# Hidden rows of a bias MLP on a third engine, and the first loads on another queue

## The chip, the cores and the metric

The kernel runs on one core of one Trainium2 chip. The metric is the device time of one execution in microseconds (us), the median of three runs. The engines are PE (TensorE), PEld (its weight loads), DVE (VectorE), ACT (ScalarE), POOL (GpSimd) and SP (SyncE, which here only issues DMAs).

## The reference, cut to what matters

Attention over 2 x 8 heads of 576 positions with a bias from a small MLP on positions, then two mixture-of-experts layers on its output. What the change touches is the bias:

```python
rel = (pos[:, None] - pos[None, :]).astype(np.float32)
psi_rel = np.log1p(np.abs(rel))
psi_i = np.log1p(np.maximum(pos[:, None].astype(np.float32), 1.0))
x = (psi_rel / psi_i)[..., None]
h = np.maximum(x @ w1 + b1, 0.0)      # 32 hidden values for each (i, j)
bias = h @ w2                         # 8 heads
scores = scores + bias.transpose(2, 0, 1)[None, :, :, :]
```

After it come the softmax, the product with V and the two layers of experts (each a relu between two matrix products, weighted by probabilities).

## The kernel before

**The bias.** Psi of row i is positive, so relu(psi_rel * w1 / psi_i + b1) is relu(psi_rel * w1 + b1 * psi_i) / psi_i. A tile `T` of 128 x 576 holds psi_rel * w1 by distance, 32 hidden values for each of four rows i, and a *hidden row* (a `hid`, made by `emit_hid`, L312 to L319) is relu(T + b1 * psi_i) for four rows i: one instruction of 128 partitions by up to 576 elements. Four hidden rows, q = 0 to 3, make a *group* g of 16 rows i; there are 36 groups. For a group, PE multiplies the four hidden rows by w2 (L330; a first matmul waits for q = 0, the next for q = 1 and so on), ACT scales the product into a staging buffer `bsts` (L359, three buffers in rotation), and SP writes that to a scratch tensor `bd` in device memory (L362). From there `load_bias` (L283 to L290) reads the bias of a whole tile of scores back, shifted row by row, as `bt`.

**Where hidden rows lie.** There are 12 places for hidden rows, three groups' worth. A place comes free when PE has multiplied what it holds, so the hidden rows of the group that is m-th in order can be made once PE is done with group m - 3. The order of the groups is 0 to 7, then 32 to 35, then 8 to 31.

**The stage ahead of the first unit.** A *unit* is one tile of 128 rows of one pair of heads in one batch: scores on PE (`emit_S`, L380), bias and maximum on DVE (`emit_max`, L398), exponentials on ACT (L411), and two units later the transposes and the product with V. Before the first unit the kernel makes eight groups in a loop of eight steps, then three groups more (groups 32 to 34); each step issues a group's matmuls and copies and then the four hidden rows of the group two later. In between it splits the first queries and keys into a high and a low part (`prep_q`, `prep_k`, L232 to L235 and L253 to L254). All of it is issued in program order on every engine: no engine overtakes a waiting instruction of its own. The first unit's maximum needs its scores, which stand on PE behind group 34, and its bias, which `load_bias(0)` reads after groups 0 to 7 are written; on SP it stands behind the write of group 32.

**Which engine makes a hidden row.** `hids(k, engs)` issues k hidden rows, those with an index in `engs` on ACT and the others on DVE. In the first stage that is q = 1 on ACT and q = 0, 2, 3 on DVE; in the three groups after it all are on DVE.

**Loads.** `load_q` and `load_k` bring the queries (`qr`) and keys (`kr`), two DMAs each, issued on POOL. POOL also zeroes the last fifth of the four V tiles (L503), and during the units it adds 1e-9 to the sums (L417), spreads the reciprocals (L423) and issues the loads of V.

**The rest.** From the fourth unit on, PE is the engine that the others feed, through attention and the 96 steps of the experts.

Of the kernel before, what the change touches and what calls it, by code (L numbers as in the profile page):

```python
# [12 lines left out]
ALU = mybir.AluOpType  # L13
# [3 lines left out]
B, H, S, D = 2, 8, 576, 64  # L17
# [31 lines left out]
def attn_moe_moe(ctx: ExitStack, tc: tile.TileContext, pack, keep, rel, qT, kT, vT, w, out):  # L49
    nc = tc.nc  # L50
    pe, ve, sc, gp, sy = nc.tensor, nc.vector, nc.scalar, nc.gpsimd, nc.sync
# [131 lines left out]
    def attention(moe):  # L183
# [12 lines left out]
        b1psi = ata.tile([128, 144], F32, name="b1psi")  # L196
# [3 lines left out]
        T = ata.tile([128, S], F32, name="T")  # L200
        V = [atb.tile([128, 5, 2 * B * D], F32, name=f"V{p}") for p in range(4)]
# [10 lines left out]
        tps_ = [(t, p) for t in (0, 4, 1, 2, 3) for p in range(4)]  # L212
        units = [(t, p, b) for t, p in tps_ for b in range(2 if t < 4 else 1)]
        U = len(units)
        kk, qq, bt, rawk, rawq = {}, {}, {}, {}, {}


        def load_k(p, b):
            if b == 0:
                x = xa.tile([128, 1280], F32, tag=f"x0{XA[p]}", name=f"kr{p}")  # L220
                rawk[p, 0], rawk[p, 1] = x[:, 0:S], x[:, S:2 * S]
            for h in range(2):
                gp.dma_start(out=rawk[p, b][64 * h:64 * h + 64], in_=kT[p, b, 0:64, S * h:S * h + S])  # L223

        lows = []

        def prep_k(p, b, hi):
            r = rawk[p, b]
            kk[p, b] = ata.tile([128, 2, S], F32R, name=f"kk{p}{b}")
            h = kk[p, b][:, 0, :]  # L230
            if hi is sc:
                sc.activation(out=h, in_=r, func=AF.Copy)  # L232
            else:
                ve.tensor_copy(h, r)
            lows.append(lambda: ve.tensor_tensor(out=kk[p, b][:, 1, :], in0=r, in1=h.bitcast(F32), op=ALU.subtract))  # L235

        def prep_lows():
            while lows:
                lows.pop(0)()

        def load_q(t, p):
            r = ata.tile([128, 256], F32, tag="qraw", name=f"qr{t}{p}", bufs=4)
            for h in range(2):
                gp.dma_start(  # L244
                    out=r[64 * h:64 * h + 64].rearrange("p (b c) -> p b c", b=2),
                    in_=qT[t, p, 0:64].rearrange("p (b h c) -> p h b c", b=2, h=2)[:, h],
                )
            rawq[t, p] = r

        def prep_q(t, p):  # L250
            r = rawq[t, p]
            a = ata.tile([128, 2, 256], F32R, tag="qq", name=f"qq{t}{p}", bufs=3)
            ve.tensor_copy(a[:, 0, :], r)  # L253
            ve.tensor_tensor(out=a[:, 1, :], in0=r, in1=a[:, 0, :].bitcast(F32), op=ALU.subtract)  # L254
            qq[t, p] = a
# [13 lines left out]
        def load_bias(i):  # L269

            t, p = tps_[i]
            n = 128 if t < 4 else 64

            src = bdram[t][2 * p:2 * p + 2].rearrange("h i v -> h (i v)")
            o = S - 1 - 128 * t
            src = src[:, o:o + n * (W - 1)].rearrange("h (i v) -> i h v", v=W - 1)[:, :, 0:S]
            at = [slice(n * z, n * z + n) for z in range(1 if t < 4 else 2)]
            if place[i] < 2:
                x = two[place[i]]
                bt[t, p] = x[:, 0:S], x[:, S:2 * S]  # L280
                mains, tails = x.rearrange("p (h c) -> p h c", h=2)[:, :, 0:512], x[:, 512:640].rearrange("p (h c) -> p h c", h=2)
                for z in at:
                    sy.dma_start(out=mains[z], in_=src[:, :, 0:512])  # L283
                    sy.dma_start(out=tails[z], in_=src[:, :, 512:S])
            else:
                x0, x1 = bt[t, p] = third
                for z in at:
                    sy.dma_start(out=x0[z], in_=src[:, 0, :])
                    sy.dma_start(out=x1[z, 64:S], in_=src[:, 1, 0:512])
                    sy.dma_start(out=x1[z, 0:64], in_=src[:, 1, 512:S])  # L290
# [6 lines left out]
        def ranges(g):  # L297
            fwd, rev = S - 16 * g, 16 * g + 16
            n = max(fwd, rev)
            return fwd, rev, n, 1 if n <= 512 else 2  # L300
# [5 lines left out]
        def emit_hid(g, eng, q):  # L306
            tt = 4 * g + q
            if started == 6:
                for i in XA[4:]:
                    x = xa.tile([128, 1280], F32, tag=f"x0{i}", name=f"hid{i}")  # L310
                    free.extend([(6, x[:, 0:S]), (6, x[:, S:2 * S])])
            place = free.pop(0)  # L312
            taken[g, q], x = place, place[1]
            n = ranges(g)[2]
            if eng is ve:
                ve.tensor_scalar(x[:, 0:n], T[:, 0:n], b1psi[:, tt:tt + 1], 0.0, op0=ALU.add, op1=ALU.max)
            else:
                sc.activation(out=x[:, 0:n], in_=T[:, 0:n], func=AF.Relu, bias=b1psi[:, tt:tt + 1])
            hid[g, q] = x  # L319
# [165 lines left out]
        kq = [(p, b) for p in range(4) for b in range(2)]  # L485
# [7 lines left out]
        busy(WARM)  # L493
        sy.dma_start(out=cst, in_=pack)
        sc.dma_start(out=T, in_=rel)
        load_q(*tps_[0])
        load_k(*kq[0])
        load_k(*kq[1])
        sy.dma_start(out=kept, in_=keep)
        load_q(*tps_[1])  # L500
        load_k(*kq[2])
        for p in range(4):
            gp.memset(V[p][:, 4, :], 0.0)  # L503
        ve.tensor_scalar(b1psi, cst[:, C_PSI:C_PSI + 144], b1col, None, op0=ALU.mult)
        ve.tensor_scalar(w2n, cst[:, C_W2:C_W2 + 32], 8.0, None, op0=ALU.mult)
        ve.tensor_scalar(T, T, w1col, None, op0=ALU.mult)
# [2 lines left out]
        order = list(range(8)) + list(range(32, NGR)) + list(range(8, 32))  # L509
        made = 0  # L510
        started = 0

        def hids(k, engs=()):
            nonlocal started
            for i in range(k):
                if started < 4 * NGR and (free or started == 6):
                    emit_hid(order[started // 4], sc if i in engs else ve, started % 4)
                    started += 1

        def groups(k):  # L520
            nonlocal made
            for _ in range(k):
                if made < NGR:
                    g = order[made]
                    emit_bias_out(g, emit_bias_mm(g))
                    made += 1

        FIRST = 8
        hids(8, (1, 5))
        for g in range(FIRST):  # L530
            groups(1)
            if g == 0:
                prep_q(*tps_[0])
            if g == 1:
                prep_k(*kq[0], ve)
                prep_lows()
            hids(4, (1,))
            if g == 3:
                load_k(*kq[3])
            if g == 4:  # L540
                prep_k(*kq[1], ve)
                prep_lows()
            if g == 6:
                load_k(*kq[4])
                load_q(*tps_[2])
# [2 lines left out]
        load_q(*tps_[3])  # L548
        prep_q(*tps_[1])
        prep_k(*kq[2], sc)  # L550
        for g in range(3):
            groups(1)
            hids(4)
            prep_lows()
            if g == 0:
                load_bias(0)
                load_bias(1)
# [7 lines left out]
        for k in range(U + 3):  # L565
            first = False
            if k < U:
                t, p, b = units[k]
# [398 lines left out]
    with tc.manual_schedule():  # L967
        attention(moe)
        moe.run()
# [69 lines left out]
```

## Time and profile before

| | |
|---|---|
| median of three runs | 1348.43 us (1348.18 to 1350.22) |
| span of the profiled execution | 1346.6 us |
| time around the span (median less span) | 1.8 us |
| PE busy | 1332.0 us, 99% of the span |
| DVE, ACT, POOL busy | 783.9, 519.0 and 434.2 us |

The span runs from the first to the last instruction of the profiled execution; its own time is that span, and the runs' median stands 1.8 us above it. A busy share of 99% for PE is over the whole span: the first 40 us are the stretch in which PE waits for others, and they are the stretch that the change touches.

### The profile page before, as it was taken

Reading aid. Unit: us, or ns where it says so; the run is one execution under the profiler, and the core shown is the slowest. Engines: PE = TensorE matmul, PEld = TensorE weight load, DVE = VectorE, ACT = ScalarE, POOL = GpSimd, SP = SyncE. Lnnn points to the kernel's source line nnn. Section 1 sums busy time; section 2 is a strip of 40 time slices with the busy share of each in tenths; the row PEclk is TensorE's granted clock in tenths of the full one; section 3 lists DMA queues with packets and bytes.
Section 4 is the critical chain, followed back from the end, with each engine's and each line's share of the span. In section 5 each row is a group of like instructions: output and inputs, shape, how many; then the busy total and the mean of one; then the engine's idle time right before and its main releaser. Section 6 shows DMA issues by size and latency. Waiting matters only on the chain.

```text
span 1346.6 us, 22479 instructions
## 1 busy us (share of the span) xinstructions
PE 1332.0 (99%) x8783; PEld 1163.1 (86%) x8783; DVE 783.9 (58%) x1771; ACT 519.0 (39%) x1230; POOL 434.2 (32%) x455
## 2 busy tenths in 40 slices
PE   8999999999999999999999999999999999999998
PEld 4677888898898988898898988998988898989887
DVE  7888977463564653765763654644735725645533
ACT  6888863341331422443342421422422413313311
POOL 4633433260440530361440530620612603504400
PEclk9999999999999999999999999999999999999999
DMA  7975421020120210020110110210210200202010
GB/s 220 240 199 145 143 64 63 32 94 1 38 88 1 63 64 1 32 75 21 63 63 1 63 63 1 80 47 1 94 32 30 92 5 32 95 0 63 32 40 32
DMA packets 34314, 84.68 MB, mean 63 GB/s; under 512 B 8864, under 2 KB 9120, under 8 KB 34208
## 3 DMA queue, kind: packets, MB, share of 16 engines
q1 hardware_dynamic: 31184, 75.60, 18.0%
q0 software_dynamic: 2880, 7.34, 2.0%
q8 instruction: 69, 1.13, 0.3%
q14 instruction: 37, 0.30, 0.1%
q10 hardware_dynamic: 144, 0.29, 0.1%
HBM read 69.97 MB, written 13.25 MB: 62 GB/s over the span
## 4 chain that ended last, share of the span: by engine, by line
PE 92%; DVE 3%; POOL 2%; issue 2%; ACT 1%; DMA 0%; SPq 0%; ACTq 0%; POOLq 0%; DVEq 0%
PE y L778 43%; PE B L699 17%; PE A L699 11%; PE C L699 11%; PE po L469 3%; PE sc L380 2%; PE tp L443 2%; PE bps L330 1%; POOL kr L223 1%; POOL qr L244 1%; DVE rows L800 0%; PE sc L431 0%; PE turn L867 0%; DMA rawb<-in_w 0%; DVE h L713 0%
## 5 line engine op out<-in xcount | busy, mean ns | idle before, releaser
L778 PE MATMUL y<-gb,h 128*128 128x512 f32 x2592 | 714.1, 395 | 0.0
L778 PEld LDWEIGHTS y<-gb,h 128*128 128x128 f32 x2592 | 450.2, 188 | 55.3
L169 POOL TENSOR_TENSOR gb<-rawb,gb 128x512 fp32r<-128x512 f32 x94 | 122.9, 1322 | 627.9 <-ACT gb L168 624.9
L707 DVE TENSOR_TENSOR u<-B,s 128x320 f32<-128x320 f32 (+1 forms) x192 | 87.8, 457 | 333.4 <-PE B L699 333.4
L710 ACT ACTIVATE h<-c 128x320 fp32r<-128x320 f32 (+1 forms) x288 | 119.7, 439 | 368.5 <-DVE c L707 367.1
L713 DVE SCALAR_TENSOR_TENSOR h<-c,h 128x320 fp32r<-128x320 f32 (+1 forms) x288 | 182.4, 650 | 53.7 <-ACT h L710 49.4
L169 POOL TENSOR_TENSOR ga<-rawa,ga 128x512 fp32r<-128x512 f32 x94 | 127.2, 1371 | 4.3 <-ACT ga L168 2.7
L169 POOL TENSOR_TENSOR ga<-wt,ga 128x512 fp32r<-128x512 f32 x94 | 107.3, 1161 | 24.5 <-ACT ga L168 15.7
L707 DVE TENSOR_TENSOR c<-C,u 128x320 f32<-128x320 f32 (+1 forms) x192 | 87.1, 454 | 37.7 <-PE C L699 33.9
L721 ACT ACTIVATE s<-A 128x320 f32<-128x320 f32 (+1 forms) x96 | 39.4, 411 | 165.6 <-PE A L699 165.3
L168 ACT ACTIVATE gb<-rawb 128x512 fp32r<-128x512 f32 x96 | 60.1, 627 | 86.0 <-DMA rawb<-in_w 86.0
L710 ACT ACTIVATE h<-A 128x320 fp32r<-128x320 f32 (+1 forms) x96 | 38.9, 405 | 137.9 <-PE A L699 137.8
L707 DVE TENSOR_TENSOR c<-B,s 128x320 f32<-128x320 f32 (+1 forms) x96 | 43.9, 457 | 73.9 <-PE B L699 72.7
L699 PE MATMUL B<-x20S,ga 128*128 128x320 f32 x384 | 66.9, 310 | 0.0
L699 PE MATMUL A<-x20A,ga 128*128 128x320 f32 x384 | 66.8, 309 | 0.0
L699 PE MATMUL C<-x20S,ga 128*128 128x320 f32 x384 | 66.7, 309 | 0.0
L699 PEld LDWEIGHTS C<-x20S,ga 128*128 128x128 f32 x384 | 61.4, 188 | 5.9 <-DVE c L707 0.2
L699 PEld LDWEIGHTS A<-x20A,ga 128*128 128x128 f32 x384 | 61.5, 188 | 5.7
L699 PEld LDWEIGHTS B<-x20S,ga 128*128 128x128 f32 x384 | 61.5, 188 | 5.8
L411 ACT ACTIVATE s<-s,stat 128x576 f32<-128x576 f32 x72 | 55.7, 774 | 18.8 <-DVE stat L398 18.6
L699 PEld LDWEIGHTS C<-x21S,ga 128*128 128x128 f32 x384 | 54.6, 188 | 8.1 <-DVE c L707 2.7
L699 PEld LDWEIGHTS A<-x21A,ga 128*128 128x128 f32 x384 | 54.7, 188 | 5.5
(183 smaller groups left out, 1915.5 us busy)
## 6 DMA issues: line engine op xcount, KB each, us to landing
rawa<-in_w SPq DMA_DIRECT2D x48, 512.0 KB, 4.0
rawb<-in_w SPq DMA_DIRECT2D x48, 512.0 KB, 4.9
bd<-bsts SPq DMA_DIRECT2D x36, 295.5 KB, 3.6
bt<-bd SPq DMA_DIRECT2D x13, 512.0 KB, 4.7
qr<-in_qT POOLq DMA_DIRECT2D x40, 64.0 KB, 3.2
kr<-in_kT POOLq DMA_DIRECT2D x16, 144.0 KB, 4.4
V<-in_vT POOLq DMA_DIRECT2D x4, 512.0 KB, 7.3
out<-rows SPq DMA_DIRECT2D x8, 256.0 KB, 2.1
```

The source lines that it names most:

```text
L168: sc.activation(out=z(0), in_=src, func=AF.Copy)
L169: lo.tensor_tensor(out=z(1), in0=src, in1=z(0).bitcast(F32), op=ALU.subtract)
L380: pe.matmul(out=o[h][c:c + n, j, 0:288], lhsT=a[d, 128 * bb + c:128 * bb + c + n], rhs=m[d, 288 * j:288 * j + 288], start=t == 4 or i == 0 ...
L411: sc.activation(out=s, in_=s, func=AF.Exp, scale=-1.0, bias=stat[u][:, h:h + 1], accum_out=stat[u][:, 2 + h:3 + h],)
L443: pe.transpose(o[:, j, :], s[:, 640 * h + 128 * j:640 * h + 128 * j + 128], ident)
L469: pe.matmul(out=o[64 * h:64 * h + 64, c0:c0 + n], lhsT=V[p][:, j, col:col + D], rhs=rhs, start=j == 0, stop=j == 4,)
L699: pe.matmul(out=ban[o], lhsT=a, rhs=x[:, z, k, :], start=not more and i == 0, stop=i == 5, skip_group_check=more,)
L707: ve.tensor_tensor(out=t[o], in0=ban[a], in1=t[b], op=ALU.add)
L710: sc.activation(out=h[f][:, 0, half, :], in_=src, func=AF.Relu)
L713: ve.scalar_tensor_tensor(out=h[f][:, 1, half, :], in0=src, scalar=0.0, in1=h[f][:, 0, half, :].bitcast(F32), op0=ALU.max, op1=ALU.subtract,)
L721: sc.activation(out=t["s1"], in_=ban["A"], func=AF.Copy)
L778: pe.matmul(out=self.y[t], lhsT=a, rhs=x, start=g == 0 and f == 0 and i == 0, stop=g == NP - 1 and f == 1 and i == 2,)
```

## The change

Four edits, all ahead of the first unit.

- Hidden rows: of every eight in a row, numbers 0 and 4 (q = 0 of every group) are made by POOL, number 5 (q = 1 of every second group) by ACT, and the other five by DVE. This goes for the first 52 hidden rows, the three last groups of the stage included.
- `load_q` and `load_k` take a queue as an argument, and the first two queries and the first three keys are issued on SP in place of POOL.
- The zeroing of V's last fifth is issued after the loop of eight steps in place of before it.
- Later loads stay on POOL, where they now stand between its hidden rows.

```diff
-        def load_k(p, b):
+        def load_k(p, b, q=gp):
...
-                gp.dma_start(out=rawk[p, b][64 * h:64 * h + 64], in_=kT[p, b, 0:64, S * h:S * h + S])
+                q.dma_start(out=rawk[p, b][64 * h:64 * h + 64], in_=kT[p, b, 0:64, S * h:S * h + S])
...
-        def load_q(t, p):
+        def load_q(t, p, q=gp):
...
-            if eng is ve:
-                ve.tensor_scalar(x[:, 0:n], T[:, 0:n], b1psi[:, tt:tt + 1], 0.0, op0=ALU.add, op1=ALU.max)
+            if eng is not sc:
+                eng.tensor_scalar(x[:, 0:n], T[:, 0:n], b1psi[:, tt:tt + 1], 0.0, op0=ALU.add, op1=ALU.max)
...
-        load_q(*tps_[0])
-        load_k(*kq[0])
-        load_k(*kq[1])
+        load_q(*tps_[0], sy)
+        load_k(*kq[0], sy)
+        load_k(*kq[1], sy)
         sy.dma_start(out=kept, in_=keep)
-        load_q(*tps_[1])
-        load_k(*kq[2])
-        for p in range(4):
-            gp.memset(V[p][:, 4, :], 0.0)
+        load_q(*tps_[1], sy)
+        load_k(*kq[2], sy)
...
-        def hids(k, engs=()):
+        def hids(k, three=False):
...
-                    emit_hid(order[started // 4], sc if i in engs else ve, started % 4)
+                    eng = {0: gp, 5: sc, 4: gp}.get(started % 8, ve) if three else ve
+                    emit_hid(order[started // 4], eng, started % 4)
...
-        hids(8, (1, 5))
+        hids(8, True)
...
-            hids(4, (1,))
+            hids(4, True)
...
+        for p in range(4):
+            gp.memset(V[p][:, 4, :], 0.0)
         for g in range(3):
             groups(1)
-            hids(4)
+            hids(4, True)
```

On POOL, from the start of the program to the first unit, the rows before were these (`qr`, `kr` are queries and keys, `V` the V tiles):

```order
L487 MEMSET ones 128x128
L244 DMA qr_126<-in_qT 64x2x128 x2
L223 DMA kr_129<-in_kT 64x576 x4
L244 DMA qr_135<-in_qT 64x2x128 x2
L223 DMA kr_138<-in_kT 64x576 x2
L503 MEMSET V_100 128x256
...
L223 DMA kr_138<-in_kT 64x576 x2
L223 DMA kr_270<-in_kT 64x576 x2
L244 DMA qr_273<-in_qT 64x2x128 x2
L223 DMA kr_270<-in_kT 64x576 x2
L244 DMA qr_290<-in_qT 64x2x128 x2
```

Now the later part of them, from the seventh hidden row to the last of the stage, reads so (`hids` and `hidS` are places of hidden rows):

```order
L223 DMA kr_138<-in_kT 64x576 x2
L316 TENSOR_SCALAR hids<-T,b1psi 128x480
L316 TENSOR_SCALAR hids<-T,b1psi 128x464
L316 TENSOR_SCALAR hidS_151<-T,b1psi 128x528
L223 DMA kr_266<-in_kT 64x576 x2
L244 DMA qr_269<-in_qT 64x2x128 x2
L316 TENSOR_SCALAR hids<-T,b1psi 128x544
L223 DMA kr_266<-in_kT 64x576 x2
L244 DMA qr_286<-in_qT 64x2x128 x2
L551 MEMSET V_100 128x256
...
L316 TENSOR_SCALAR hids<-T,b1psi 128x560
```

Ten DMA issues have left the head of POOL's queue, 13 hidden rows have come into it, and the q = 0 row of group 34 (the 128x560 one) now stands behind eight DMA issues and four memsets that follow the row of group 32 (128x528), with only the row of group 33 (128x544) between.

On SP, the start of the program (`cst` holds the constants, `kept` the identity and gate weights):

```order
 L494 DMA cst<-in_pack 128x214
+L244 DMA qr_126<-in_qT 64x2x128 x2
+L223 DMA kr_129<-in_kT 64x576 x4
 L499 DMA kept<-in_keep 128x196
+L244 DMA qr_135<-in_qT 64x2x128 x2
+L223 DMA kr_138<-in_kT 64x576 x2
 L362 DMA bd_104<-bsts 16x8x591 x8
```

Ten issues have come ahead of the first write of a group; from that write on SP's rows are those of before.

## Rows read from the trace of the kernel before

**Rows 1.** The page's first line.

```profile
span 1346.6 us, 22479 instructions
```

**Rows 2.** Windows: length, busy PE, PEld, DVE, ACT, POOL, then PE's clock.

```profile
4.80:28.60 23.80, 19.62 (x166) 8.46 (x165) 22.20 (x52) 18.18 (x34) 11.03 (x19) 0.93 0.71 205
...
39.50:330.00 290.50, 289.41 (x2607) 239.83 (x2608) 203.23 (x552) 180.06 (x447) 102.59 (x163) 1.00 0.38 109
```

**Rows 3.** Timeline of DVE: start, length, instruction [idle before it and releaser].

```profile
31.10 0.76 DVE L398 CUSTOM_DVE_ANT_0 s<-sc,bt 128x576 f32<-128x576 f32 x1 [2.60 <-DMA bt<-bd]
```

**Rows 4.** Timelines of SP, ACT and PE ahead of it.

```profile
26.46 0.39 SPq L283 DMA_DIRECT2D bt<-bd  x1
...
18.78 1.05 ACT L359 ACTIVATE bsts<-bps,cst 128x496 f32<-128x496 f32 x2 [0.99 <-DMA bd<-bsts]
...
20.45 0.93 PE L330 MATMUL bps<-hids,w2n 128*32 128x464 f32 x1 [1.55 <-ACT hids L318]
```

**Rows 5.** DVE's groups of instructions by line, 4.8 to 28.6 us.

```profile
L316 DVE TENSOR_SCALAR hidS<-T,b1psi 128x560 f32<-128x560 f32 (+6 forms) x21 | 9.4, 506 | 0.0
L316 DVE TENSOR_SCALAR hids<-T,b1psi 128x448 f32<-128x448 f32 (+7 forms) x21 | 9.3, 495 | 0.3 <-PE bps L330 0.3
```

**Rows 6.** Timeline of DVE and, last, of POOL.

```profile
6.88 1.18 DVE L316 TENSOR_SCALAR hidS<-T,b1psi 128x560 f32<-128x560 f32 x2
...
14.86 1.22 DVE L316 TENSOR_SCALAR hids<-T,b1psi 128x480 f32<-128x480 f32 x3
...
17.54 0.82 DVE L316 TENSOR_SCALAR hidS<-T,b1psi 128x464 f32<-128x464 f32 x2
...
22.62 0.93 DVE L316 TENSOR_SCALAR hidS<-T,b1psi 128x560 f32<-128x560 f32 x2
...
26.96 1.54 DVE L316 TENSOR_SCALAR hids<-T,b1psi 128x448 f32<-128x448 f32 x4
...
7.16 1.80 POOL L503 MEMSET V<- 128x256 f32 x4
```

**Rows 7.** POOL's arithmetic by line, whole span: shortest, median and longest, ns.

```profile
L417 POOL TENSOR_SCALAR stat<-stat x36: 203/213/798, 33.6 to 178.2; 128x2 f32<-128x2 f32 x36
L423 POOL COPY spread<-stat x36: 287/290/697, 38.7 to 178.7; 128x128 f32<-128x128 f32 x36
L169 POOL TENSOR_TENSOR gb<-rawb,gb x94: 1275/1298/1572, 154.4 to 1259.2; 128x512 fp32r<-128x512 f32 x94
```

**Rows 8.** The same view of a DVE line in the experts.

```profile
L713 DVE SCALAR_TENSOR_TENSOR h<-c,h x288: 412/492/1575, 189.0 to 1336.3; 128x320 fp32r<-128x320 f32 x72, 128x256 fp32r<-128x256 f32 x72
L713 DVE SCALAR_TENSOR_TENSOR h<-A,h x96: 407/445/492, 186.4 to 1331.5; 128x320 fp32r<-128x320 f32 x48, 128x256 fp32r<-128x256 f32 x48
```

**Rows 9.** POOL's groups of instructions by line, 0 to 16 us.

```profile
L223 POOL DMA_DIRECT2D kr<-in_kT x12 | 7.2, 605 | 0.0
L244 POOL DMA_DIRECT2D qr<-in_qT x8 | 5.7, 711 | 0.4 <-issue 0.4
```

**Rows 10.** Timeline of PE: end of group 5, start of group 34, first scores.

```profile
15.90 0.59 PE L330 MATMUL bps<-hidS,w2n 128*32 128x496 f32 x3
...
25.53 0.43 PE L330 MATMUL bps<-hids,w2n 128*32 128x280 f32 x2 [0.39 <-ACT bsts L359]
...
28.59 1.06 PE L380 MATMUL sc<-kk,qq 64*128 64x288 f32 x12
```

**Rows 11.** Windows, columns as in rows 2.

```profile
16.50:20.40 3.90, 1.10 (x9) 0.23 (x8) 3.90 (x10) 2.85 (x7) 0.00 (x0) 1.00 0.73 240
20.40:24.00 3.60, 3.55 (x24) 0.86 (x24) 2.81 (x7) 3.21 (x8) 0.00 (x0) 0.53 0.64 170
```

**Rows 12.** DMA issues at 10 to 12 and 23 to 25 us, last: us to landing.

```profile
bd<-bsts SPq DMA_DIRECT2D x1, 295.5 KB, 5.6
...
bd<-bsts SPq DMA_DIRECT2D x1, 295.5 KB, 3.0
```

**Rows 13.** POOL's sequencer in the chain that ended last.

```profile
15.82 0.06 POOLq L417 x2
```

More of the change, by code (lines that the diff above doesn't have):

```diff
@@ L239, in prep_lows @@
                 lows.pop(0)()
-        def load_q(t, p):
+        def load_q(t, p, q=gp):
             r = ata.tile([128, 256], F32, tag="qraw", name=f"qr{t}{p}", bufs=4)
             for h in range(2):
-                gp.dma_start(
+                q.dma_start(
                     out=r[64 * h:64 * h + 64].rearrange("p (b c) -> p b c", b=2),
```

## The prediction

> **What bounds the kernel now.** I read the stages first (windows), then asked what the first unit waits for (DVE's timeline at the first maximum), and followed that wait back through the timelines of SP, ACT and PE. From 39.5 us on PE is busy 289.41 of the next 290.50 us; in the stage that makes the bias, 4.8 to 28.6 us, only 19.62 of 23.80 [rows 2]. So a shift of the first unit should move the end one for one, and nothing else that the change does can move it. The first maximum starts at 31.10, after 2.60 us in which DVE waits for the bias `bt` [rows 3]. Back from there: SP issues that load at 26.46, once group 7 is written; group 7's first matmul starts at 20.45, after a wait of 1.55 us for its hidden row on ACT; and that row stands on ACT behind the copy of group 5, which starts at 18.78 because its staging buffer is still being written out [rows 4]. DVE, busy 22.20 of 23.80 us [rows 2], is the busiest engine of the stage, but it is not what group 7 waited for: its last row of that group ended at 17.54 + 0.82 = 18.36 [rows 6]. DVE's share looks like the bound; the waits say it has some 2 us of slack.
>
> **What a POOL row takes.** The trace has no such instruction on POOL. The nearest with one input: 128x2 takes 213 ns, the copy of 128x128 290 ns (medians), 0.61 ns an element, so 0.21 + 574 x 0.61 = 0.56 us for 576 elements as the lower bound. The nearest of this length has two inputs: 1.30 us for 512, 1.46 for 576, the upper bound [rows 7]. I take 0.85, nearer to the copy, since the row has one input, and above it, since it does two operations on each element. By the Trainium skill (GPSIMD Engine Reference, "Elementwise — side-by-side cycle accounting") a tight loop on POOL does 1.8 cycles an element at 1.2 GHz, an estimate of 0.86 us and some 0.2 of start, by which the sum below would come out about 1 us later.
>
> **What it takes from DVE.** Two DVE rows of 128x560 took 1.18 us while POOL's memsets ran, 0.93 with POOL idle: 0.13 lost per row beside a memset of 0.45 [rows 6]. In the experts, DVE's instruction with both inputs in SBUF goes from 412 to 1575 ns, its twin with one input in PSUM never beyond 492 [rows 8], and beside it run POOL's subtractions of 1.3 us; a 128x2 operation of POOL that takes 203 ns at best took up to 798 [rows 7]. So the two engines hold something from each other. I charge DVE what POOL's row has beyond its start (0.85 - 0.2 = 0.65), less about 0.1 of DVE's own start that passes meanwhile, as with the memsets: 0.55 a row, bounds 0.25 and 1.15 by the two ends above.
> By the Trainium skill (SBUF — State Buffer, "Who interferes with whom") DVE's two-port operations, tensor_scalar among them, and a POOL operation share one port pair, and whoever comes second waits for the whole instruction. The rows on both sides agree. With the whole 0.85 charged, DVE below would be ready at 33.7 in place of 29.8 and the prediction 1351.0.
>
> **DVE's account up to the first maximum.** Before, 42 of the 52 hidden rows are DVE's (21 + 21) [rows 5], and its last one ends at 26.96 + 1.54 = 28.50 [rows 6]. After, numbers 0 and 4 of each eight give POOL 13, number 5 gives ACT 6 (10 before), and DVE keeps 33. Nine rows less at 0.40 each (four of 128x448 in 1.54, four of 128x560 in about twice 0.93 less overlap: a start every 0.36 to 0.42 [rows 6]) is -3.6. Thirteen POOL rows at 0.55 is +7.2. The memsets and DMA issues that stood beside some five of the early rows, 0.13 each, go: -0.7. Some 1.6 us in which DVE was idle [rows 2] take up the same amount. 28.5 - 3.6 + 7.2 - 0.7 - 1.6 = 29.8, before 31.1: not the bound. The bounds give 25.9 and 37.6.
>
> **The bias.** Through group 7, POOL makes 8 rows, DVE 20 in place of 24: 8 x 0.55 - 4 x 0.40 - 0.7 = +2.1, so DVE is done with group 7 at 20.5, when PE began it before (20.45). Its matmuls then ran at a clock of 0.53 [rows 11]. ACT gives up every second row but keeps group 7's. The write of group 7 took 3.0 us with no load beside it, that of group 1, among POOL's loads, 5.6 [rows 12]; the loads now stand later, near group 7. I take no net change for `bt`: 0, bounds -2.5 and +2.6.
>
> **POOL's queue.** This is the new path. PE's first scores come behind group 34, whose q = 0 row stands on POOL behind eight DMA issues and four memsets. Start: PE was done with group 5 at 15.90 + 0.59 = 16.5 [rows 10], and POOL's row of group 32 needs that. DVE's rows of group 5 ended at about 14.9, when those of group 6 began [rows 6]; now 6 x 0.55 - 3 x 0.40 - 0.7 = 1.4 later, 16.3, and PE 1.0 after it: 17.3. Then three POOL rows at 0.85 + 0.2 of waiting for DVE, 3.2; four issues for keys at 0.605 and four for queries at 0.711 [rows 9], 5.3; four memsets at 0.45 [rows 6], 1.8: group 34's row is there at 27.6. From the start of group 34 to the end of the first scores PE took 28.59 + 1.06 - 25.53 = 4.1 us [rows 10]: 31.7, which is 0.6 later than the 31.1 of before. And PE has then idled some 4 us. Before, it was busy 1.10 of 3.90 us from 16.5 and ran the next 3.60 us at a clock of 0.53, close to the 1.2 GHz level [rows 11]; if that comes again, 1.7 of the 4.1 us is done twice as slowly. I take most of it, 1.4: 33.1, +2.0 against 31.1. Bounds: with the short row, no waiting for DVE and full clock, 28.2, and `bt` decides; with the long row, group 5 at 19.9, 6.0 for the rows, 5.3, 1.8, 4.1 and 1.7, 38.8: +7.7.
>
> **What costs nothing.** SP's ten new issues, at about the 0.39 us of its load at 26.46 [rows 4], end near 6 us, ahead of its first write of a group, which no hidden row made after 4.8 can reach before 7. The early queries and keys are on DVE's list after its first six hidden rows, so 2 us of DVE's work covers them; if that were gone, a late key would hold DVE. V's zeroing is wanted only in the units; its 1.8 us is charged on POOL above.
>
> **The sum.** The profiled execution is 1346.6 us of span [rows 1], the median 1348.43, 1.8 around the span. 1346.6 + 2.0 = 1348.6 of span, 1350.4 by the median. A measurement here can tell about 0.2%, 2.7 us, from no change.
>
> **The rivals.**
> 1. *Faster: the waits for the staging buffers go.* Before, the copy of group 5 started at 18.78, 0.99 us late for its buffer [rows 4]; without POOL's loads among the writes (5.6 to 3.0 [rows 12]) group 7 comes up to 1.9 earlier, and 0.6 more at full clock. It decides if a POOL row costs DVE no more than it saves, 0.40, and POOL's queue reaches group 34 by 24.5. For it speaks the POOL row at the copy's rate; against it, the queue's 7.1 us of issues and memsets. 1348.4 - 2.2 = 1346.2.
> 2. *Nothing moves*: DVE's and POOL's accounts both end below 31.1 and `bt` lands as before, 1348.4. It needs the clock to stay up at group 34.
> 3. *DVE and POOL in series.* A POOL row nearer to 1.3 us: DVE's account ends near 36 and POOL's queue near 38, 1355. For it speaks that all long POOL rows in the trace are at that rate, against it that they have two inputs.
> 4. *POOL starts late.* Its sequencer has two instructions at 15.82 [rows 13] ahead of its first arithmetic, and no work for 17 us after, so a start-up could hide there; now its first row is wanted where the stage starts, at 4.8 [rows 2], and nothing hides it. If it takes until 7, the first group is 2.1 us late; POOL has little slack to make it up: up to 1352.5. The Trainium skill (GPSIMD Engine Reference, "Instruction dispatch") gives the first call after a library is loaded about 6 us; no row here shows it.
>
> **How the numbers follow.** The forecast, a POOL queue that makes the first scores 0.5 to 4.5 us late, 0.45 (its own range 1348.9 to 1352.9); rival 1, 0.17; rival 2, 0.15; rival 3, 0.16; rival 4, 0.07. The range leaves out about half of rivals 1 and 3: 1346.4 to 1354.8. Faster by over 0.2% is half of rival 1, 0.08. Slower by over 0.2% is 0.18 of the forecast (2.7 to 4.5 us late), rival 3 and most of rival 4: 0.39. The rest, 0.53, is within 0.2%.
>
> **What would show it.** Right: POOL's L316 rows near 0.85 us; DVE's rows beside them stretched by half a microsecond; PE waiting on POOL ahead of group 34, a clock near 0.5 after it, and the first maximum released by PE's scores near 33 with the same 1.8 us around the span. Wrong: DVE's rows as short as before beside POOL's; the first maximum still released by `bt`; PE waiting on POOL at the first groups (rival 4); or POOL rows of 1.3 us.

## The result, and the profile after

The changed kernel takes 1362.03 us (median of 5 runs, 1361.04 to 1362.31); the kernel before, run beside it, 1350.22 (1348.18 to 1351.74). The ratio is 1.0091, with a 95% interval of 1.008 to 1.0102 (estimated from the runs, so not quite the quotient of the two medians): slower by 0.9%, some 12 us. Against the 1348.15 and 1348.44 us that the kernel before has in the experiments below it is 13.6 to 13.9 us. The profiled execution has a span of 1360.5 us, 13.9 more than [rows 1].

The first maximum on DVE, the row that answers to [rows 3], in DVE's timeline of the changed kernel (start, length, instruction, idle before it and its releaser):

```profile
44.38 0.76 DVE L398 CUSTOM_DVE_ANT_0 s<-sc,bt 128x576 f32<-128x576 f32 x1 [7.37 <-PE sc L380]
```

It starts 13.3 us later than before, so nearly all of the 13.9 us is lost ahead of it. It is released by PE's scores and no longer by the bias `bt`. The two stages ahead of it, as windows with the columns of [rows 2], the first being that of [rows 2]:

```profile
4.80:28.60 23.80, 15.35 (x116) 3.91 (x115) 22.32 (x35) 11.83 (x23) 23.77 (x15) 0.71 0.53 145
28.60:39.50 10.90, 3.65 (x32) 1.20 (x32) 5.62 (x8) 2.55 (x5) 10.86 (x13) 0.53 0.90 250
```

POOL is busy 23.77 of 23.80 us (11.03 before) and 10.86 of the next 10.90. PE is busy 15.35 us in the first stage (19.62 before) and runs at a clock of 0.71, then 0.53 (the 1.2 GHz level is 0.5). The waits up to 55 us (engine and line, what it waited for, us in total, times, longest) say who waits for POOL:

```profile
PE bps L330 <- POOL hids L316: 13.9, 6, 4.3
...
PE bps L330 <- POOL hidS L316: 1.6, 3, 0.7
...
DVE hids L316 <- PE bps L330: 3.9, 2, 2.8
```

POOL's timeline shows why. It answers to [rows 6, 7, 9]:

```profile
4.78 5.35 POOL L316 TENSOR_SCALAR hids<-T,b1psi 128x576 f32<-128x576 f32 x2 [3.85 <-DVE T L504]
10.11 2.68 POOL L316 TENSOR_SCALAR hidS<-T,b1psi 128x544 f32<-128x544 f32 x1
12.77 4.53 POOL L316 TENSOR_SCALAR hids<-T,b1psi 128x528 f32<-128x528 f32 x2
17.29 2.14 POOL L316 TENSOR_SCALAR hidS<-T,b1psi 128x496 f32<-128x496 f32 x1
...
20.70 3.87 POOL L316 TENSOR_SCALAR hids<-T,b1psi 128x480 f32<-128x480 f32 x2
24.55 2.24 POOL L316 TENSOR_SCALAR hidS<-T,b1psi 128x528 f32<-128x528 f32 x1
26.75 1.17 POOL L223 DMA_DIRECT2D kr<-in_kT  x2
27.91 1.29 POOL L244 DMA_DIRECT2D qr<-in_qT  x2
29.23 3.01 POOL L316 TENSOR_SCALAR hids<-T,b1psi 128x544 f32<-128x544 f32 x1
32.20 1.11 POOL L223 DMA_DIRECT2D kr<-in_kT  x2
33.30 1.20 POOL L244 DMA_DIRECT2D qr<-in_qT  x2
34.49 1.08 POOL L551 MEMSET V<- 128x256 f32 x4
35.55 2.29 POOL L316 TENSOR_SCALAR hids<-T,b1psi 128x560 f32<-128x560 f32 x1
37.84 2.20 POOL L316 TENSOR_SCALAR hidS<-T,b1psi 128x576 f32<-128x576 f32 x1
40.02 1.77 POOL L316 TENSOR_SCALAR hids<-T,b1psi 128x448 f32<-128x448 f32 x1
```

From 4.78 us on POOL runs without a gap; nothing releases its rows but its own queue. A row takes 1.77 to 3.0 us, on average 2.31 over the 13 (the ten groups come to 30.1 us). The last two ran after DVE had made its last hidden row of the stage: alone, 576 elements take 2.20 us and 448 take 1.77. For the mean length of the 13 rows, 524 elements, that gives an estimate of 2.03 us, so most of the length is POOL's own and some 0.3 us a row comes from running beside DVE. The row of group 34 (128x560) is done at 35.55 + 2.29 = 37.84. PE's timeline from there, which answers to [rows 10] (L491 are products that the kernel makes only to keep PE busy, before as after), and the same stretch as a window with the columns of [rows 2]:

```profile
37.90 0.68 PE L330 MATMUL bps<-hids,w2n 128*32 128x280 f32 x2 [3.56 <-POOL hids L316]
...
39.92 3.43 PE L491 MATMUL po<-ones 128*128 128x128 f32 x16
...
43.28 1.06 PE L380 MATMUL sc<-kk,qq 64*128 64x288 f32 x12
```

```profile
37.90:44.34 6.44, 6.44 (x45) 4.73 (x45) 0.00 (x0) 1.59 (x3) 3.89 (x2) 0.62 0.64 170
```

From group 34's start to the end of the first scores PE takes 43.28 + 1.06 - 37.90 = 6.44 us, 2.3 more than the 4.12 of before: its matmuls take 0.68 where they took 0.43, after 3.56 us without work, and the clock of the stretch is 0.62 where it was 1.00 (25.53 to 29.65 us before). DVE's groups from 4.8 to 43 us answer to [rows 5] (busy us, mean ns of one):

```profile
L316 DVE TENSOR_SCALAR hidS<-T,b1psi 128x560 f32<-128x560 f32 (+6 forms) x18 | 12.9, 766 | 0.3 <-PE bps L330 0.3
L316 DVE TENSOR_SCALAR hids<-T,b1psi 128x576 f32<-128x576 f32 (+6 forms) x15 | 10.0, 712 | 3.9 <-PE bps L330 3.9
```

33 rows take 22.9 us, 0.69 each; before it was 42 in 18.7, 0.445 each. So 22.9 - 33 x 0.445 = 8.2 us is lost, 0.63 for each of 13 POOL rows, or 0.75 for each of the 11 that had rows of DVE beside them. It is not what ends the stage: DVE itself waits 3.9 us here.

### The profile page after: what moved, and what is told of

Its sections match the earlier page's. It is cut to its first block, busy times and chain, and to the rows that moved or that the text cites. A ratio compares the mean times of both kernels' runs of the same rounds, so it can differ in the third digit from the quotient of the medians.

```text
span 1360.5 us, 22499 instructions
## 1 busy us (share of the span) xinstructions
PE 1335.4 (98%) x8783; PEld 1162.6 (85%) x8783; DVE 792.9 (58%) x1762; ACT 516.9 (38%) x1226; POOL 456.4 (34%) x458
## 4 chain that ended last, share of the span: by engine, by line
PE 91%; DVE 5%; POOL 2%; ACT 1%; issue 1%; DMA 1%; SPq 0%; ACTq 0%; DVEq 0%; POOLq 0%
PE y L779 42%; PE B L700 16%; PE C L700 11%; PE A L700 11%; PE po L469 3%; PE sc L380 2%; PE tp L443 2%; PE bps L330 2%; POOL hids L316 1%; DVE wt L165 1%; DVE h L714 1%; PE po L491 1%; POOL hidS L316 0%; DVE rows L801 0%; PE sc L431 0%
```

## The experiments

**The theory, A**: a hidden row on POOL is some 2.7 times as long as the prediction took it; 13 of them in order, with the eight DMA issues and four memsets between, make POOL the bound of the stage, and its last row ahead of group 34 sets the first scores. **The rivals**: that the loads moved to SP or the late zeroing cost the time; that DVE's loss beside POOL does, or the rows that ACT no longer makes; that the POOL row is long only for its place or its operands; that PE's idle clock carries the loss; and that the plan would lose with short rows too.

**1. No hidden rows on POOL.** The rows are dealt out to DVE and ACT as before; the loads on SP and the late zeroing stay.

```diff
-                    eng = {0: gp, 5: sc, 4: gp}.get(started % 8, ve) if three else ve
-                    emit_hid(order[started // 4], eng, started % 4)
+                    emit_hid(order[started // 4], sc if i in engs else ve, started % 4)
...
-        hids(8, True)
+        hids(8, (1, 5))
...
```

> Hidden rows as before (q = 1 on ACT, the others on DVE), the moved loads and the later zeroing kept. Theory A (POOL's 13 hidden rows at 2.2 to 3.0 us each are the whole loss): the first maximum returns to about 31 us or a little ahead, the time is 1346 to 1350 us. Rival B (the loads on SP or the late zeroing carry a part of the 12 us): over 1353 us.

Measured: 1348.86 us against 1348.15, ratio 1.0005 (0.9994 to 1.0016). DVE's timeline has the first maximum a little earlier than before:

```profile
30.13 0.76 DVE L398 CUSTOM_DVE_ANT_0 s<-sc,bt 128x576 f32<-128x576 f32 x1 [2.75 <-DMA bt<-bd]
```

The loads and the zeroing cost nothing that can be measured. The 1.0 us by which the first unit comes earlier is nearly all given back: the span is 1346.3 us, 0.3 less.

**2. The hidden rows alone.** The opposite: POOL has its 13 rows, and the loads and memsets stand at the head of its queue again.

```diff
-        load_q(*tps_[0], sy)
-        load_k(*kq[0], sy)
-        load_k(*kq[1], sy)
+        load_q(*tps_[0])
+        load_k(*kq[0])
+        load_k(*kq[1])
...
+        for p in range(4):
+            gp.memset(V[p][:, 4, :], 0.0)
...
-        for p in range(4):
-            gp.memset(V[p][:, 4, :], 0.0)
```

> Only POOL's hidden rows: all loads back on POOL, the zeroing back ahead of the stage. Theory A (POOL's queue in series): ten loads and the zeroing stand ahead of POOL's first row, which comes at about 9 us in place of 4.8; the 1.1 us of late zeroing goes; first maximum 46 to 48 us, time 1363 to 1367 us. Rival B (the moved loads hurt): 1355 us or less.

Measured: 1363.42 us, ratio 1.0107 (1.0091 to 1.0122), the first maximum on DVE at 45.82:

```profile
45.82 0.76 DVE L398 CUSTOM_DVE_ANT_0 s<-sc,bt 128x576 f32<-128x576 f32 x1 [7.28 <-PE sc L380]
```

The rows alone bring the whole loss; clearing POOL's queue ahead of them gives 1.4 us of the first maximum back.

**3. What a row on POOL takes, by form.** Behind the last output tile of the kernel before, with the other engines idle, POOL does eight forms on 128x512 from SBUF to SBUF, twice (`sx` and `so` are 128x512, `col` is a column: one value for each partition).

```diff
...
+        for _ in range(2):
+            gp.tensor_scalar(so, sx, col, 0.0, op0=ALU.add, op1=ALU.max)
+            gp.tensor_scalar(so, sx, col, None, op0=ALU.add)
+            gp.tensor_scalar(so, sx, 0.5, 0.0, op0=ALU.add, op1=ALU.max)
+            gp.tensor_scalar(so, sx, 0.5, None, op0=ALU.add)
+            gp.tensor_scalar(so, sx, 0.0, None, op0=ALU.max)
+            gp.tensor_scalar(so, sx, 0.5, 0.25, op0=ALU.mult, op1=ALU.add)
+            gp.tensor_copy(so, sx)
+            gp.tensor_tensor(out=so, in0=sx, in1=sx, op=ALU.add)
```

> The kernel before, with eight forms of a POOL instruction of 128x512 appended after the last output tile, each twice, on idle engines: two operations with a column operand (the hidden row's form), one operation with a column, two and one with constants, a maximum alone, multiply-add with constants, a copy, a sum of two inputs. From POOL's rows that ran alone after the change (2.20 us for 576, 1.77 for 448) the first form takes 1.98 us. Theory C1 (the second operation costs): the one-operation forms take about half, 1.0 to 1.2 us, with or without the column. Theory C2 (the column operand costs): the forms with constants take 1.0 to 1.2 and one operation with a column about 2. Theory C3 (every tensor_scalar on POOL costs this): all near 2 us, the copy 0.5 to 0.6. The time has no meaning beside the kernel before but for some 20 us at its end.

Measured, POOL's timeline, in the order of the diff (the second round differs by 0.01 at most):

```profile
1346.80 2.01 POOL L974 TENSOR_SCALAR forms<-rows,kept 128x512 f32<-128x512 f32 x1 [76.61 <-DVE rows L800]
1348.91 1.58 POOL L975 TENSOR_SCALAR forms<-rows,kept 128x512 f32<-128x512 f32 x1
1350.58 1.92 POOL L976 TENSOR_SCALAR forms<-rows 128x512 f32<-128x512 f32 x1
1352.59 1.49 POOL L977 TENSOR_SCALAR forms<-rows 128x512 f32<-128x512 f32 x1
1354.16 1.49 POOL L978 TENSOR_SCALAR forms<-rows 128x512 f32<-128x512 f32 x1
1355.73 0.62 POOL L979 TENSOR_SCALAR forms<-rows 128x512 f32<-128x512 f32 x1
1356.42 0.61 POOL L980 COPY forms<-rows 128x512 f32<-128x512 f32 x1
1357.11 1.04 POOL L981 TENSOR_TENSOR forms<-rows 128x512 f32<-128x512 f32 x1
```

The row's own form takes 2.01 us with every other engine idle, so its length needs neither its place in the stage nor DVE beside it. None of the three explanations came out as stated: the column in place of a constant costs 0.09 us and the second operation 0.43, but one addition or one maximum by itself already takes 1.49, while a multiplication and an addition together take 0.62, a copy's time. Why POOL has a fast and a slow kind, no run here shows.

**4. Half the rows.** POOL makes the first of every eight, 7 in all, and DVE the rest.

```diff
-                    eng = {0: gp, 5: sc, 4: gp}.get(started % 8, ve) if three else ve
+                    eng = {0: gp, 5: sc}.get(started % 8, ve) if three else ve
```

> One hidden row of eight on POOL in place of two (7 in place of 13), DVE takes the others. Theory A (POOL's queue in series): up to group 34 it has 6 rows x 2.3 + 10 issues x 0.62 + 1.1 of zeroing = 21 us from 4.8, so group 34's row is there at 26, first scores at 30 to 31; the time is 1347 to 1352 us. Rival D (any row on POOL holds DVE for all of its 2.2 us, whatever the queue): DVE, 39 rows x 0.41 + 7 x 2.2 + 4 of splits from 4.8, ends at 40, the time is 1357 us or more.

Measured: 1352.71 us, ratio 1.0031 (1.0022 to 1.0041), the first maximum at 34.88, some 4 us later than theory A said and far below its rival. PE still waits for POOL, twice, for 6.5 us:

```profile
PE bps L330 <- POOL hids L316: 6.5, 2, 4.5
```

A's direction holds and its number was too low: group 34 starts on PE at 29.11, when POOL's row is there, and not at 26, and from there to the end of the first scores PE takes 5.7 us in place of 4.12, at a clock of 0.70 (29.1 to 34.8 us).

**5. The five later loads off POOL's queue.** All 13 rows stay on POOL; SP issues these loads too.

```diff
-                load_k(*kq[3])
+                load_k(*kq[3], sy)
...
-        load_k(*kq[5])
-        load_q(*tps_[3])
+        load_k(*kq[5], sy)
+        load_q(*tps_[3], sy)
```

> The changed kernel with its 13 hidden rows on POOL, and the five loads that stood between them issued on SP as well. Theory A (POOL's queue in series): the eight issues of 1.2 to 1.3 us a pair, 6.0 us up to group 34's row, leave the queue; the first maximum comes at about 38 to 39 in place of 44.4, the time is 1355 to 1358 us. Rival E (the issues were hidden, and POOL's rows wait for PE's places or for DVE instead): 1360 us or more.

Measured: 1357.05 us, ratio 1.0061 (1.0046 to 1.0076), the first maximum at 39.51, 4.9 us earlier than in the changed kernel. Ten issues are off the queue; the eight ahead of group 34's row had taken 4.8 us there (1.17 + 1.29 + 1.11 + 1.20 in the timeline above), so what leaves the queue leaves the time. The rest of the loss stays with the rows.

**6. A cheap form.** POOL's 13 rows as the fast form of experiment 3; their relu is left out.

```diff
+            if eng is gp:
+                gp.tensor_scalar(x[:, 0:n], T[:, 0:n], 1.0, b1psi[:, tt:tt + 1], op0=ALU.mult, op1=ALU.add)
...
```

> The changed kernel with POOL's 13 rows in the form of a multiplication by 1 and an addition of the column: the relu is left out of those rows. On idle engines such a form with constants took 0.62 us for 512 in place of 2.01. Theory A with the prediction's own sum (only the price of a row was wrong): at 0.65 to 0.9 us a row the first maximum comes at 30.5 to 33, the time is 1347.5 to 1351 us. Rival F (the number of POOL rows and their hold on DVE matter, not their length): 1356 us or more.

Measured: 1348.34 us against 1348.44, ratio 1.0002 (0.9992 to 1.0011). POOL's rows by source line (shortest, median, longest, ns):

```profile
L316 POOL TENSOR_SCALAR hids<-T,b1psi x9: 735/910/1088, 4.7 to 25.3; 128x560 f32<-128x560 f32 x2, 128x576 f32<-128x576 f32 x1, 128x528 f32<-128x528 f32 x1, 128x512 f32<-128x512 f32 x1
...
L316 POOL TENSOR_SCALAR hidS<-T,b1psi x4: 816/865/907, 6.6 to 24.5; 128x544 f32<-128x544 f32 x1, 128x496 f32<-128x496 f32 x1, 128x528 f32<-128x528 f32 x1, 128x576 f32<-128x576 f32 x1
```

That is about the 0.85 us that the prediction took, in the same place beside the same work, and the loss is gone: the length of the row is the whole cause. ACT's rows are those of the changed kernel, so they are not the cause, and DVE's loss beside short rows is not either. The plan also gains nothing with short rows. DVE's timeline and the chain, in order of time, say what decides then:

```profile
32.80 0.76 DVE L400 CUSTOM_DVE_ANT_0 s<-sc,bt 128x576 f32<-128x576 f32 x1 [3.32 <-DMA bt<-bd]
```

```profile
22.36 6.19 DMA bd<-bsts
...
28.75 0.39 SPq L283 DMA_DIRECT2D bt<-bd  x1
```

Group 34's row is done at 24.46 and no longer decides; `bt` does, as before, but its load is issued at 28.75 in place of 26.46, behind a write of the bias that takes 6.2 us (3.0 before [rows 12]). POOL's loads now run beside that write; that they are what makes it longer is my reading, and no run takes them away with these rows. The first maximum is 1.7 us later in this execution, whose span (1348.9) belongs to the longest of the ten runs; in the median of the ten nothing of it shows, and I leave that open.

**7. Half the rows, loads first.** Experiment 4 with POOL's five later loads at the head of its queue.

```diff
+        load_k(*kq[3])
+        load_k(*kq[4])
+        load_q(*tps_[2])
+        load_k(*kq[5])
+        load_q(*tps_[3])
...
```

> One row in eight on POOL, and the five later loads at the head of POOL's queue, ahead of its first row, the zeroing behind. Theory A: POOL's queue is 7.7 us of loads, then 5 rows x 2.4, 1.1 to 1.6 of zeroing and group 34's row, which is there at 24 to 25; the first maximum waits for the bias again, 30 to 32, the time is 1347 to 1350 us, no better than before. Rival G (a POOL row costs DVE more than it saves): the maximum later than 33, over 1351 us.

Measured: 1350.53 us, ratio 1.0012 (1.0002 to 1.0021), the first maximum at 32.55 and released by PE's scores:

```profile
32.55 0.76 DVE L398 CUSTOM_DVE_ANT_0 s<-sc,bt 128x576 f32<-128x576 f32 x1 [1.10 <-PE sc L380]
```

A little above what theory A said, and not by its path: the first maximum does not wait for the bias. POOL's row of group 34 is done at 23.00 + 2.42 = 25.42, and what PE then waits for is DVE, whose last rows of that group end at 27.12 + 1.23 = 28.35 (22.62 + 0.93 = 23.55 before [rows 6]). POOL's and DVE's timelines:

```profile
23.00 2.42 POOL L316 TENSOR_SCALAR hids<-T,b1psi 128x560 f32<-128x560 f32 x1 [0.43 <-PE bps L330]
```

```profile
27.12 1.23 DVE L316 TENSOR_SCALAR hidS<-T,b1psi 128x560 f32<-128x560 f32 x2
```

The chain runs back from there over DVE's rows and PE's first groups to POOL's first row, which the loads ahead of it put at 7.21 us in place of 4.78. So this run lies between theory A and rival G. Seven slow rows don't pay even with every load out from between them.

**8. PE kept busy ahead of groups 33 and 34.** The changed kernel, with idle matmuls (`busy`) on PE while it waits for POOL.

```diff
         for g in range(3):
+            if g:
+                busy(14)
             groups(1)
```

> The changed kernel with 14 more warm-up products on PE ahead of group 33 and ahead of group 34 (some 3.6 us each, while PE would wait for POOL). Theory A with a clock term: PE, no longer idle, keeps its 2.4 GHz level, group 34 to the end of the first scores takes 4.1 to 4.5 us in place of 6.4, the first maximum comes at 42 to 42.5, the time is 1358.5 to 1360.5 us. Rival H (the clock has no part, POOL's queue alone sets the end): unchanged at 1362 us, or later.

Measured: 1359.93 us, ratio 1.0088 (1.0072 to 1.0105); the span is 1357.6 us, 2.9 less than that of the changed kernel. PE's timeline, and the window from the start of group 34 to the end of the first scores:

```profile
37.68 0.43 PE L330 MATMUL bps<-hids,w2n 128*32 128x280 f32 x2
...
40.74 1.06 PE L380 MATMUL sc<-kk,qq 64*128 64x288 f32 x12
```

```profile
37.68:41.80 4.12, 4.12 (x46) 3.17 (x45) 0.00 (x0) 1.58 (x3) 3.65 (x2) 1.00 0.87 224
```

Group 34 starts 0.2 us earlier than in the changed kernel and its first scores end 40.74 + 1.06 - 37.68 = 4.12 us later, as long as before the change. The clock there is 1.00 in place of 0.62. So 6.44 - 4.12 = 2.3 us of the loss is the clock to which PE had fallen while it waited, and the rest, 11.5 us by this run (1359.93 against 1348.44), stays with POOL's queue.

## Why the prediction was wrong

**The step that failed is "What a POOL row takes".** It took 0.85 us, with bounds of 0.56 and 1.46; measured are 2.20 us alone for 576 elements and 2.31 on average in the stage, where the rows are 448 to 576 elements long. The bounds came from the nearest rows, a copy and a subtraction of two inputs, and experiment 3 shows that neither bounds an addition and a maximum: a copy of 512 takes 0.61, the two-input addition 1.04, the row's form 2.01. "Nearer to the copy, since the row has one input" ordered the forms by their inputs, and POOL doesn't. The estimate by the Trainium skill (GPSIMD Engine Reference, "Elementwise — side-by-side cycle accounting"), 0.86 us and some start, was too short in the same way; the measurement decides.

**"POOL's queue" was the right path with one wrong term.** Group 32's row started at 24.55, not 17.3, because the POOL rows ahead of it end only there; the three rows took 2.24 + 3.01 + 2.29 = 7.5 us in place of 3.2; the eight issues 4.8 (5.3) and the memsets 1.1 (1.8). Together 37.84 for group 34's row, where I had 27.6: 10.2 us, all of it row length, since the other two terms were too dear by 1.2. Behind it stand 6.4 us on PE where I had 4.1 + 1.4 = 5.5: experiment 8 puts the clock's part at 2.3. 10.2 + 0.9 = 11.1 of the 11.3 us by which the first maximum missed 33.1. The step's upper bound, 38.8, was also added up short: it leaves out the 1.0 us of PE behind group 5 that the forecast itself has; with it the bound is 39.8, still 4.6 us ahead of the 44.38 measured.

**"What bounds the kernel now"**: the shift came one for one, 13.3 us at the first maximum and 13.9 in the span. In small steps it is not exact: 1.0 us earlier was worth 0.3 (experiment 1).

**"What it takes from DVE"**: 0.55 was forecast for a POOL row, 0.63 was measured (0.75 without the two rows that ran alone), and 0.44 beside the short rows of experiment 6, whose DVE groups from 4.8 to 28.6 us come to 19.5 us for 31 rows:

```profile
L318 DVE TENSOR_SCALAR hidS<-T,b1psi 128x560 f32<-128x560 f32 (+6 forms) x18 | 10.2, 617 | 0.0
L318 DVE TENSOR_SCALAR hids<-T,b1psi 128x576 f32<-128x576 f32 (+6 forms) x13 | 9.3, 761 | 0.0
```

(19.5 - 31 x 0.445 = 5.7, over 13.) There DVE's last hidden row of the stage ends at 29.49 (29.8 forecast). The sum was nearly right, the reasoning only in part: a POOL row 2.6 times as long cost DVE 1.4 to 1.7 times as much. So DVE does not lose what POOL's row has beyond its start. Nor does the rule of the Trainium skill (SBUF — State Buffer, "Who interferes with whom") that the second comer waits for the whole instruction hold for these rows. In the changed kernel POOL's row of 128x496 stands from 17.29 to 19.43 us; three of DVE's rows start after it and are done before it:

```profile
17.36 1.62 DVE L316 TENSOR_SCALAR hids<-T,b1psi 128x480 f32<-128x480 f32 x3 [1.08 <-PE bps L330]
```

**"The bias"**: 0, with a bound of +2.6. It could not be seen after the change, where POOL's queue hid it; experiment 6, where rows have the length that I took, shows 28.75 - 26.46 = 2.3 us later, as I read it by the loads that "now stand later, near group 7". So with a row of 0.85 us the first maximum would have come at 32.8, near the 33.1 forecast, but by luck: released by `bt`, with POOL's queue done at 24.46, 3.1 us ahead of the 27.6 worked out. The time would have been that of before, 1348.34, where I had 1350.4.

**"What costs nothing"**: right (experiment 1), though SP's ten issues end at 8.2 us and not near 6, as its timeline shows, still ahead of its first write at 9.94:

```profile
6.97 1.24 SPq L223 DMA_DIRECT2D kr<-in_kT  x2
9.94 20.11 SPq L362 DMA_DIRECT2D bd<-bsts  x9
```

**The rivals.** Rival 3, "DVE and POOL in series", had the direction and the condition, a longer row; it stopped at 1.3 us and 1355 because nothing in the trace was longer. Rival 4 fell: POOL's first row starts at 4.78, when `T` is there. Rivals 1 and 2 needed rows that hold `bt` where it was or bring it earlier; experiment 6 has such rows, and the time is that of rival 2, though its loads make `bt` later.

## What to carry to other kernels

An instruction that the trace does not show on an engine has no safe bounds from other forms on that engine: time the form itself, or leave the upper end open. When work is handed to an idle engine, add up its queue in order, issues and memsets included, against the time at which each of its results is wanted; an engine that makes one row of every group is in the path of all of them. And an engine that waits for it can pay twice, as PE did here with its clock.

## What the runs showed of the hardware that was not expected

On POOL an addition or a maximum with a scalar on 128x512 f32 took 1.49 us and both together 1.92, or 2.01 with a column; a multiplication and an addition took 0.62, a copy 0.61, an addition of two inputs 1.04. So which operation it is mattered more than how many operations or inputs the instruction has. And POOL rows 2.6 times as long took only 1.4 to 1.7 times as much from DVE beside them (0.63 to 0.75 against 0.44 us a row). PE's waits for POOL cost 2.3 us beyond the waits themselves, by the clock that they left behind (0.62 against 1.00).
